# Attention row maxima: every third pair of score products split into two steps of 256 keys that share one bank, with the order written over two key tiles

## The chip, the core and the metric

The kernel runs on one core of one Trainium2 chip. The metric is the device time of one execution in microseconds (us). Engines are named as in the profile: PE is the matrix engine (PEld its weight loads), DVE the vector engine, ACT the scalar engine, POOL GpSimd, SP the engine whose queue issues nearly all DMAs.

## The reference

```python
x = A_x                                     # 1 x 2048 x 640, 32 heads of 20
x = x + A(layernorm(x))                     # attention: softmax(q k^T / sqrt(20)) v, then wo
x = x + B(layernorm(x))                     # squared ReLU MLP, 640 -> 1536 -> 640
x = x + A(layernorm(x))                     # the same weights again
x = x + B(layernorm(x))
```

All of it is float32. The softmax is the usual one: for each query row of each head the largest score over all 2048 keys is subtracted before the exponential. The kernel must therefore know the row maximum of every query before it forms that query's weights, and it forms every score twice: once to find the maxima, once to be exponentiated.

## The kernel before, in words

**Split numbers.** Inputs of most products are held as a rounded high part and the rest. For queries and keys three copies of the 20 numbers of a head stand below one another, so one product with a depth of 60 rows gives an accurate score. 60 rows fit into one half of the 128 rows of PE. One half (partitions 0 to 63) serves the even head of a pair, the other half (64 to 127) the odd head, and matmuls on the two halves run beside each other.

**Blocks and key tiles.** Attention goes over 32 blocks per layer (`NBLK`): 8 groups of 4 heads times 4 blocks of 512 queries. A block goes over 16 key tiles of 128 keys. For every key tile PE does

- four score products, depth 62, 128 keys by 512 queries (`score`, L565). The two rows beyond 60 carry the negative row maximum in two parts. ACT takes the exponential of each (L572) into a weights tile `e`;
- some products for maxima of a later block (`smax`, L493, with the matmul at L481): 128 queries by 512 keys. DVE reduces each bank to one column of `mx` (TENSOR_REDUCE, L493);
- the weighted sum (`pv`, L577): four heads side by side on 32 columns each, two passes each, accumulated in bank 7 over the 16 key tiles. It uses the weights of the key tile before the one whose scores have just been issued.

**Banks.** Scores rotate over banks 0 to 3, products for maxima over banks 4, 5 and 6 (`sm_ring`), the weighted sum has bank 7. A product for maxima waits until DVE has reduced what stood in its bank.

**At the end of a block** `finish` (L590) copies bank 7 out on DVE, and the reciprocal of the sums and the division follow on POOL. Once all maxima of a block are there, `mrows_max` (L525) takes the maximum over the columns of its `mx` tile, and `mrows` (L536) transposes the result. Both stand on DVE. POOL and SP then send the rows into the query tiles.

**The order.** Work on PE, DVE and ACT is issued in the order of a table, `ORDERS`, one string for eight key tiles, picked by the number of pairs of products for maxima that are due (`pairs`, 12 to 16; the same (query rows, keys) for both halves of the rows are a pair). In this program the string of 12 is picked all 62 times in each layer. Its letters: `a` and `b` are a score product on the lower and the upper half of the rows, `m` and `n` a product for maxima on the lower and the upper half, `V` the weighted sum. Eight key tiles hold 16 `a`, 16 `b`, 12 `m`, 12 `n` and 8 `V`. So between two `V` stand seven matmuls, four of them on one half of the rows and three on the other. The last block of a layer has no maxima left and is done in another way (`both_heads`, L1091).

**Before and between** stand the projections of q, k and v (`qkv`, with the first blocks' maxima), wo and the MLP, which the change leaves as they are.

A dependency that the framework does not see is added by `after(later, earlier)`. The projections already use it: where both halves of the rows add to one bank, a copy of one number on ACT (`mark_t`, L333) waits for the first half's last matmul, and the other half's first matmul waits for that copy.

Of the kernel before, what the change touches and what calls it, by code (L numbers as in the profile page):

```python
# [16 lines left out]
P = 128  # L17
# [7 lines left out]
QB = 512  # L25
NQB = S // QB
NG = H // 4
NKT = S // P
# [3 lines left out]
LEAST = -3.0e38  # L32
# [7 lines left out]
def tile_layers(  # L40
# [40 lines left out]
    banks = psum.tile([P, 8, 512], F32, tag="banks", name="banks")  # L81
# [215 lines left out]
    xt_, keys = {}, {}  # L297
# [125 lines left out]
    k_t, q_t, v_t, mx_t, kept = {}, {}, {}, {}, {}  # L423
# [46 lines left out]

    def maxima(t):
        if t not in mx_t:
            mx_t[t] = small.tile([P, 4, 4, 4], F32, tag="mx", bufs=14, name=name("mx"))
            if t in PARTLY:
                nc.vector.memset(mx_t[t], LEAST)
        return mx_t[t]

    def by_queries(dst, t, p, sub, c, par):

        b = 64 * par  # L480
        nc.tensor.matmul(  # L481
            dst,
            q_t[t][b : b + 60, p, sub * P : (sub + 1) * P],
            k_t[t // NQB, c][b : b + 60, p, :],
            start=True,
            stop=True,
        )

    def smax(ring, t, p, sub, c, par):

        dst = ring("sm")
        by_queries(dst, t, p, sub, c, par)
        nc.vector.tensor_reduce(  # L493
            maxima(t)[:, 2 * par + p, sub, c : c + 1], dst, axis=AX.X, op=ALU.max
        )

    def step_one(t, p, sub, x, par):
# [25 lines left out]
    def mrows_max(t):  # L523
        nm = nms[t % 2]
        nc.vector.tensor_reduce(  # L525
            nm[:, :16].rearrange("p (h s) -> p h s", h=4),
            mx_t.pop(t),
            axis=AX.X,
            op=ALU.max,
            negate=True,  # L530
        )
# [152 lines left out]
    def qkv(first, x_src, rest, scores):  # L684
# [275 lines left out]
        15: "anbmnanbaabmbnammbnaVbmbmmbVmbananVanmbanVnambmbVanbmnaVnmbaanVmbbanmV",  # L960
        14: "mbbbanmbbmambmVanannaVmbnaaanVbmabnmVanbmbmbVnaanmbVmabmbanVbmannaVn",
        13: "baanmbVmbanambbnbmVanbmnaVnaabnmbVanbmaanVnmbbanaVmnbmabVabbmmnaVm",
        12: "naambbmVanmbambVbmannabVnabnmabVabnmbanVbbmnanaVbmmbaanVbmbmnaaV",
    }

    def attention(first, x_src, first_rows):
# [1 line left out]
        es_of = {}  # L968
        e_n.clear()
        weights.extend(slot([P, 2, QB], F32, "e") for _ in range(6))  # L970
        st_n, sm_n = [0, 0], [0, 0]
        state = {"begun": -1, "done": 0, "acc": None, "debt": 0}
        sm_ring = Ring(4, 5, 6)
        todo = [
            (t, p, sub, c)
            for t in range(NBLK)
# [11 lines left out]
        ends = {x[0]: n for n, x in enumerate(todo)}  # L988
        blocks = sorted(ends)
        firsts = {todo[0][0]: 0, **{t: ends[s] + 1 for s, t in zip(blocks, blocks[1:])}}  # L990
        over = {t for t in range(NBLK) if t not in ends and t not in done}
        rows = {"next": min(t for t in range(NBLK) if t not in done), "at": None}

        def begin(i):

            t, u = divmod(i, NKT)
            g, qb = divmod(t, NQB)
            if u == 1:
                q_t.pop(t - 1, None)
                if t + 2 < NBLK and t + 2 not in q_t:  # L1000
                    load_q(t + 2)
            if u % 4 == 1 and qb == 0:
                k_t.pop((g - 1, u // 4), None)
                for h in (0, 1, 2, 3) if g else (0, 1, 2):
                    if g + h < NG and (g + h, u // 4) not in k_t:
                        load_k(g + h, u // 4, True)
                if g and g + 3 >= NG:
                    del kept[(g - 1) % 4, u // 4]
            if t == 1 and u % 4 == 1:
                load_k(3, u // 4, True)  # L1010
            if u in (2, 10) and qb == NQB - 1 and g + 1 < NG:
                load_v(g + 1, u // 8)
            if first and t < 16 and u % 6 == 3:
                prep_job()
            if first and t < 16 and u == 8:
                for sp in (w_o, w_1, w_2):
                    sp.save_full()
                    sp.past(sp.count, sp.got)
            if (t, u) in loads:
                loads[t, u]()  # L1020
            if t == NBLK - 1 and u == 12:
                first_rows.extend(row_tile(x_src, i) for i in range(4))
            if i in split:
                split.pop(i)()

        def op(o):
            if o in "ab":
                par = "ab".index(o)
                i, p = divmod(st_n[par], 2)
                if i >= last:  # L1030
                    return
                st_n[par] += 1
                if i > state["begun"]:
                    state["begun"] = i
                    begin(i)
                score(i // NKT, i % NKT, 2 * p + par, es_of.setdefault(i, {}))
            elif o in "mn":
                par = "mn".index(o)
                n = sm_n[par]
                if n == len(todo):  # L1040
                    return
                t, p, sub, c = todo[n]
                if n == firsts[t] and par == 0:
                    for s in blocks[blocks.index(t) :][:2]:
                        if s not in q_t:
                            load_q(s)
                if (t // NQB, c) not in k_t or t not in q_t:
                    return
                sm_n[par] += 1
                smax(sm_ring, t, p, sub, c, par)  # L1050
                if n == ends[t] and min(sm_n) > n:
                    over.add(t)
                    if t * NKT > state["begun"] + 2 * NKT:
                        del q_t[t]
# [46 lines left out]

        def pairs():

            n, i = min(sm_n), state["begun"] + 1
# [15 lines left out]
        spare = 0  # L1120
        while state["done"] < wide:
            for o in ORDERS[pairs()]:
# [3 lines left out]
                        both_heads(spare // 2 - 1)  # L1126
                else:
                    op(o)
        assert min(sm_n) == len(todo) and spare == 4
        for p in (0, 1, 0):  # L1130
            both_heads(p)
        while state["done"] < last:
# [360 lines left out]
```

## Time and profile before

| | |
|---|---|
| median of 3 runs | 3583.39 us (3582.76 to 3584.02) |
| profiled execution, span from first to last instruction | 3581.5 us |
| PE busy | 3569.0 us (100%) |
| DVE busy | 2753.5 us (77%) |
| ACT busy | 2647.3 us (74%) |
| POOL busy | 805.2 us (22%) |
| products for maxima (L481 on `k`), count | 3586 |
| reductions (L493), count | 3076 |
| attention's key tile loop, by the weighted sums' first and last start | 312.5 to 3174.0 us, in two stretches |

The profiled execution's own time is its span and the little that lies around it: the runs stand 1.3 to 2.5 us above the span. Attention fills two stretches, from about 310 to 1393 us and from about 2090 to 3174 us. Times of instructions in timeline rows are in us from the start of the span. A matmul's row begins with its weight load when that load is not hidden, and its end is modelled. Rows of DVE and ACT include the time in which a result is written out, while the next instruction has already begun.

### The profile page before, as it was taken

Reading aid. Unit: us, or ns where it says so; the run is one execution under the profiler, and the core shown is the slowest. Engines: PE = TensorE matmul, PEld = TensorE weight load, DVE = VectorE, ACT = ScalarE, POOL = GpSimd, SP = SyncE. Lnnn points to the kernel's source line nnn. Section 1 sums busy time; section 2 is a strip of 40 time slices with the busy share of each in tenths; the row PEclk is TensorE's granted clock in tenths of the full one; section 3 lists DMA queues with packets and bytes.
Section 4 is the critical chain, followed back from the end, with each engine's and each line's share of the span. In section 5 each row is a group of like instructions: output and inputs, shape, how many; then the busy total and the mean of one; then the engine's idle time right before and its main releaser. Section 6 shows DMA issues by size and latency. Waiting matters only on the chain.

```text
span 3581.5 us, 67667 instructions
## 1 busy us (share of the span) xinstructions
PE 3569.0 (100%) x25560; PEld 2121.6 (59%) x25560; DVE 2753.5 (77%) x5085; ACT 2647.3 (74%) x5146; POOL 805.2 (22%) x880
## 2 busy tenths in 40 slices
PE   9999999999999999999999999999999999999999
PEld 7896343333334335999988954333334433369998
DVE  8778999999999993455567789999999999824443
ACT  3778999999999995122237789999999999942221
POOL 6531434211211211111153201211211211211110
PEclk9999999999999999999999999999999999999999
DMA  9765555323211136834477652232232211367221
GB/s 305 274 230 167 168 157 155 105 69 81 57 44 51 46 95 204 262 99 115 134 275 244 192 149 70 62 81 60 66 79 54 52 39 45 112 216 248 74 80 39
DMA packets 377397, 452.58 MB, mean 126 GB/s; under 512 B 176642, under 2 KB 223746, under 8 KB 377070
## 3 DMA queue, kind: packets, MB, share of 16 engines
q1 hardware_dynamic: 376254, 445.89, 41.6%
q8 instruction: 201, 3.29, 0.4%
q10 hardware_dynamic: 816, 2.36, 0.2%
q14 instruction: 126, 1.03, 0.1%
HBM read 273.83 MB, written 174.30 MB: 125 GB/s over the span
## 4 chain that ended last, share of the span: by engine, by line
PE 96%; DVE 2%; DMA 1%; issue 0%; ACT 0%; POOL 0%; SPq 0%; ACTq 0%; DVEq 0%
PE banks L577 28%; PE banks L565 20%; PE banks L481 16%; PE banks L293 13%; PE banks L331 10%; PE banks L1259 9%; DVE mx L493 1%; PE banks L1091 1%; DMA q<-d_qk 0%; ACT e L1098 0%; DVE bst L244 0%; DVE xnT L257 0%; DVE x L252 0%; DMA d_qk<-ev 0%; PE banks L408 0%
## 5 line engine op out<-in xcount | busy, mean ns | idle before, releaser
L572 ACT ACTIVATE e<-banks 128x512 f32<-128x512 f32 x3968 | 2049.4, 604 | 61.1 <-PE banks L481 1.7
L493 DVE TENSOR_REDUCE mx<-banks 128x1 f32<-128x512 f32 x3076 | 1929.6, 683 | 208.4 <-PE banks L481 137.2
L481 PE MATMUL banks<-k,q 60*128 60x512 f32 x3586 | 1244.3, 427 | 1.0 <-DMA q<-d_qk 0.5
L565 PE MATMUL banks<-q,k 62*128 62x512 f32 x3968 | 1118.7, 434 | 0.4 <-DVE mx L510 0.4
L577 PE MATMUL banks<-e,vg 128*32 128x512 f32 x8192 | 1091.0, 605 | 1.5 <-ACT e L1098 1.5
L565 PEld LDWEIGHTS banks<-q,k 62*128 62x128 f32 x3968 | 584.4, 185 | 657.8 <-ACT e L572 625.6
L481 PEld LDWEIGHTS banks<-k,q 60*128 60x128 f32 x3586 | 582.0, 184 | 283.1 <-DVE mx L493 210.8
L510 DVE CUSTOM_DVE_ANT_0 rl<-banks,rl 128x512 f32<-128x512 f32 x510 | 332.6, 688 | 101.6 <-PE banks L481 91.0
L331 PE MATMUL banks<-xnT,wqk 64*128 64x512 f32 x2400 | 379.7, 394 | 0.3 <-ACT mark_t L333 0.3
L1244 ACT ACTIVATE r<-banks,b_t 128x512 f32<-128x512 f32 x96 | 66.2, 689 | 419.7 <-PE banks L293 418.3
L577 PEld LDWEIGHTS banks<-e,vg 128*32 128x32 f32 x8192 | 161.1, 108 | 360.2 <-issue 333.1
L502 ACT ACTIVATE rl<-banks 128x512 f32<-128x512 f32 x510 | 270.8, 597 | 98.9 <-PE banks L481 93.6
L1259 PE MATMUL banks<-w,h 128*128 128x320 f32 x2304 | 340.4, 309 | 0.0
L1259 PEld LDWEIGHTS banks<-w,h 128*128 128x128 f32 x2304 | 339.2, 188 | 1.2
L293 PE MATMUL banks<-xnT,w 128*128 128x512 f32 x1440 | 329.4, 389 | 0.0
L331 PEld LDWEIGHTS banks<-xnT,wqk 64*128 64x128 f32 x2400 | 286.4, 185 | 34.3 <-issue 2.4
L293 PEld LDWEIGHTS banks<-xnT,w 128*128 128x128 f32 x1440 | 269.6, 188 | 55.3
L271 POOL CAST mr<-nt 128x32 fp32r<-128x32 f32 x64 | 13.4, 209 | 1143.5 <-DVE nt L536 1143.5
L621 POOL TENSOR_TENSOR few<-few,minus_t 128x16 f32<-128x16 f32 x62 | 179.8, 2900 | 215.6 <-DMA few<-d_s 213.7
L331 PE MATMUL banks<-wv,xnT 64*128 64x320 f32 x1920 | 199.2, 307 | 0.9 <-ACT mark_t L333 0.9
L331 PEld LDWEIGHTS banks<-wv,xnT 64*128 64x128 f32 x1920 | 186.5, 185 | 2.7 <-ACT mark_t L333 1.4
L1245 DVE TENSOR_TENSOR r<-r 128x512 f32<-128x512 f32 x96 | 74.3, 774 | 124.0 <-ACT r L1244 124.0
(86 smaller groups left out, 2010.8 us busy)
## 6 DMA issues: line engine op xcount, KB each, us to landing
q<-d_qk SPq DMA_DIRECT2D x242, 240.0 KB
d_qk<-ev SPq DMA_DIRECT2D x80, 512.0 KB
k<-d_qk SPq DMA_DIRECT2D x152, 240.0 KB
x<-d_x SPq DMA_DIRECT2D x84, 320.0 KB
d_qk<-ev SPq DMA_DIRECT2D x80, 256.0 KB
d_o<-ot SPq DMA_DIRECT2D x248, 80.0 KB
ot<-d_o SPq DMA_DIRECT2D x38, 512.0 KB
d_v<-v SPq DMA_DIRECT2D x32, 512.0 KB
```

The costliest lines, as they stand in the source:

```text
L293: nc.tensor.matmul(dst, a, b, start=(n == 0), stop=(n == last))
L331: m = nc.tensor.matmul(ch["dst"][:, :width], *pair, start=first, stop=last)
L481: nc.tensor.matmul(dst, q_t[t][b : b + 60, p, sub * P : (sub + 1) * P], k_t[t // NQB, c][b : b + 60, p, :], start=True, stop=True,)
L493: nc.vector.tensor_reduce(maxima(t)[:, 2 * par + p, sub, c : c + 1], dst, axis=AX.X, op=ALU.max)
L502: nc.scalar.activation(res, dst, AF.Relu)
L510: nc.vector.tensor_tensor_reduce(out=r, in0=dst, in1=r, scale=1.0, scalar=LEAST, op0=ALU.add, op1=ALU.max, accum_out=maxima(t)[:, 2 * par ...
L565: nc.tensor.matmul(dst, k_t[t // NQB, kt // 4][b : b + 62, p, (kt % 4) * P : (kt % 4 + 1) * P], q_t[t][b : b + 62, p, :], start=True, stop ...
L572: nc.scalar.activation(es[p][:, par, :], dst, AF.Exp, scale=SCALE)
L577: nc.tensor.matmul(acc[32 * h : 32 * h + 32, :], v_t[t // NQB, kt // 8][:, kt % 8, 32 * h : 32 * h + 32], es[p][:, par, :], start=(kt == 0 ...
L621: nc.gpsimd.tensor_tensor(few, few, minus_t, op=ALU.pow)
L1245: nc.vector.tensor_mul(r, r, r)
L1259: nc.tensor.matmul(dst[:, :HALF], hs[f][:, hx, i * P : (i + 1) * P], w_2.piece(at_2(f0 + f, hw, hf)), start=(f == 0 and (hx, hw) == THREE[0]),
```

## The change

Of every three pairs of products for maxima two stay as they were, and the third is done in two steps (`u` and `w` in the table). Step one takes the first 256 keys, step two the last 256. In each step `u` puts the lower half's 128 x 256 product into the left half of a bank and `w` the upper half's into the right half of the same bank. Then one DVE reduction over 2 x 256 elements gives two columns of `mx`, one for each of the two heads. Matmuls on two halves of the rows must not write one bank at once, so a one-element memset on DVE (`done_t`, called mark below) waits for `u`, and `w` waits for the mark.

The string of 12 becomes four times a string over two key tiles. In the first of them stand u n a b a b m w, in the second b u a n m b a w: three and a half products of 512 columns on each half of the rows. The bank of `u` is held until `w`'s reduction is done and then goes to the end of the list `turn` of the three banks.

`mx` gets eight columns in place of four for each head and part of the rows, so `mrows_max` reduces 128 x 128 numbers in place of 128 x 64. The four new columns are set to a very small number by a memset on POOL (`two_columns`), called for a block and the one after it when the block's first product is taken up.

```diff
-            mx_t[t] = small.tile([P, 4, 4, 4], F32, tag="mx", bufs=14, name=name("mx"))
+            mx_t[t] = small.tile([P, 4, 4, 8], F32, tag="mx", bufs=14, name=name("mx"))
...
+    def two_columns(t):
+
+        if t not in halved:
+            halved.add(t)
+            nc.gpsimd.memset(maxima(t)[:, :, :, 4:], LEAST)
+
+    def smax_half(bank, t, p, sub, c, half, par, earlier=None):
+
+        w = QB // 2
+        dst = bank[:, par * w : (par + 1) * w]
+        m = by_queries(dst, t, p, sub, c, par, slice(half * w, (half + 1) * w))
+        if earlier is None:
+            mark = nc.vector.memset(done_t, 0.0)
+            after(mark, m)
+            return mark
+        after(m, earlier, "matmuls on two halves of the rows write to one bank in turn")
+        nc.vector.tensor_reduce(
+            maxima(t)[:, p : p + 3 : 2, sub, c + 4 * half],
+            bank.rearrange("q (r k) -> q r k", r=2),
+            axis=AX.X,
+            op=ALU.max,
+        )
...
-            mx_t.pop(t),
+            mx_t.pop(t)[:, :, :, : 8 if t in halved else 4],
...
-        12: "naambbmVanmbambVbmannabVnabnmabVabnmbanVbbmnanaVbmmbaanVbmbmnaaV",
+        12: "unababmwVbuanmbawV" * 4,
...
+            elif o == "u":
+                if parts or next_pair(parts):
+                    x = parts.pop(0)
+                    bank = turn.pop(0)
+                    opened.append((bank, x, smax_half(banks[:, bank, :], *x, 0)))
+            elif o == "w":
+                if opened:
+                    bank, x, mark = opened.pop()
+                    smax_half(banks[:, bank, :], *x, 1, mark)
+                    turn.append(bank)
+                    did(x[0])
```

How the instructions stand then. On PE, in the middle of the first layer's attention, two key tiles before; L565 are scores, L481 products for maxima, L577 the weighted sum:

```order
L481 MATMUL banks<-k_4704,q_12529 128x512
L565 MATMUL banks<-q_12607,k_4699 128x512 x2
L481 MATMUL banks<-k_4704,q_12529 128x512 x2
L565 MATMUL banks<-q_12607,k_4699 128x512 x2
L577 MATMUL banks<-e_4746,vg_12626 32x512 x2
L577 MATMUL banks<-e_4745,vg_12626 32x512 x2
L565 MATMUL banks<-q_12607,k_4699 128x512 x2
L481 MATMUL banks<-k_4704,q_12529 128x512 x2
L565 MATMUL banks<-q_12607,k_4699 128x512 x2
L481 MATMUL banks<-k_4704,q_12529 128x512
L577 MATMUL banks<-e_4748,vg_12626 32x512 x2
L577 MATMUL banks<-e_4747,vg_12626 32x512 x2
```

And two key tiles now, where L591 are scores, L603 the weighted sum, and L481 with 128x256 the two half products `u` and `w`:

```order
L481 MATMUL banks<-k_4788,q_11342 128x256
L481 MATMUL banks<-k_4788,q_11342 128x512
L591 MATMUL banks<-q_10840,k_4488 128x512 x4
L481 MATMUL banks<-k_4788,q_11342 128x512
L481 MATMUL banks<-k_4788,q_11342 128x256
L603 MATMUL banks<-e_4745,vg_10679 32x512 x2
L603 MATMUL banks<-e_4744,vg_10679 32x512 x2
L591 MATMUL banks<-q_10840,k_4488 128x512
L481 MATMUL banks<-k_4788,q_11342 128x256
L591 MATMUL banks<-q_10840,k_4488 128x512
L481 MATMUL banks<-k_4788,q_11342 128x512 x2
L591 MATMUL banks<-q_10840,k_4488 128x512 x2
```

Seven matmuls of 512 columns have become six of 512 and two of 256, and the last matmul ahead of the weighted sum is always `w`.

On DVE around the end of a block, before: L493 are the reductions, L590 is the copy of bank 7, L525 and L536 are the row maxima and their transposition of a later block.

```order
L493 TENSOR_REDUCE mx_7653<-banks 128x1 x36
L590 COPY o_7976<-banks 128x512
L493 TENSOR_REDUCE mx_7653<-banks 128x1 x12
L525 TENSOR_REDUCE nm_89<-mx_5770 128x16
L536 STREAM_TRANSPOSE nt_8068<-nm_89 128x32
L493 TENSOR_REDUCE mx_7653<-banks 128x1 x8
```

And now, around a copy (L616; L512 is the mark, L516 the reduction of a shared bank):

```order
L512 MEMSET done_t 1x1
L493 TENSOR_REDUCE mx_8431<-banks 128x1 x2
L516 TENSOR_REDUCE mx_8431<-banks 128x2
L616 COPY o_9382<-banks 128x512
L512 MEMSET done_t 1x1
L493 TENSOR_REDUCE mx_8431<-banks 128x1 x2
L516 TENSOR_REDUCE mx_8431<-banks 128x2
```

Per key tile DVE has three reductions as before, and a mark ahead of them. The mark stands directly behind the copy (and, four key tiles later, directly behind the row maxima and their transposition), ahead of the reductions of its key tile. There are 984 marks, 984 reductions of a shared bank and 2092 of the old kind in the program.

More of the change, by code (lines that the diff above doesn't have):

```diff
@@ L472, in maxima, with by_queries @@
         if t not in mx_t:
-            mx_t[t] = small.tile([P, 4, 4, 4], F32, tag="mx", bufs=14, name=name("mx"))
+            mx_t[t] = small.tile([P, 4, 4, 8], F32, tag="mx", bufs=14, name=name("mx"))
             if t in PARTLY:
-                nc.vector.memset(mx_t[t], LEAST)
+                nc.vector.memset(mx_t[t][:, :, :, :4], LEAST)
         return mx_t[t]
-    def by_queries(dst, t, p, sub, c, par):
+    def by_queries(dst, t, p, sub, c, par, keys=slice(0, QB)):
         b = 64 * par
-        nc.tensor.matmul(
+        return nc.tensor.matmul(
             dst,
             q_t[t][b : b + 60, p, sub * P : (sub + 1) * P],
-            k_t[t // NQB, c][b : b + 60, p, :],
+            k_t[t // NQB, c][b : b + 60, p, keys],
             start=True,
@@ L494, in smax @@
             maxima(t)[:, 2 * par + p, sub, c : c + 1], dst, axis=AX.X, op=ALU.max
+        )
+    halved = set()
+    done_t = cpool.tile([1, 1], F32, name="done_t")
+    def two_columns(t):
[16 more added lines that the diff above has]
+            op=ALU.max,
         )
@@ L970, in attention, with sm_ring @@
         weights.extend(slot([P, 2, QB], F32, "e") for _ in range(6))
-        st_n, sm_n = [0, 0], [0, 0]
+        st_n, sm_n = [0, 0], [0]
+        full, parts, opened = [[], []], [], []
+        halved.clear()
         state = {"begun": -1, "done": 0, "acc": None, "debt": 0}
-        sm_ring = Ring(4, 5, 6)
+        turn = [4, 5, 6]
+        def sm_ring(label):
+            return banks[:, turn[0], :]
         todo = [
@@ L991, in attention @@
         over = {t for t in range(NBLK) if t not in ends and t not in done}
+        to_do = {t: 2 * sum(x[0] == t for x in todo) for t in blocks}
         rows = {"next": min(t for t in range(NBLK) if t not in done), "at": None}
@@ L1024, in begin, with next_pair, did @@
                 split.pop(i)()
+        def next_pair(queues):
+            n = sm_n[0]
+            if n == len(todo):
+                return False
+            t, p, sub, c = todo[n]
+            if n == firsts[t]:
+                for s in blocks[blocks.index(t) :][:2]:
+                    if s not in q_t:
+                        load_q(s)
+                    two_columns(s)
+            if (t // NQB, c) not in k_t or t not in q_t:
+                return False
+            sm_n[0] += 1
+            if queues is parts:
+                parts.extend((t, p, sub, c, half) for half in range(2))
+            else:
+                for q in full:
+                    q.append((t, p, sub, c))
+            return True
+        def did(t):
+            to_do[t] -= 1
+            if not to_do[t]:
+                over.add(t)
+                if t * NKT > state["begun"] + 2 * NKT:
+                    del q_t[t]
         def op(o):
@@ L1038, in op @@
                 par = "mn".index(o)
[L1039 to L1054, printed above, removed]
+                if full[par] or next_pair(full):
+                    x = full[par].pop(0)
+                    smax(sm_ring, *x, par)
+                    turn.append(turn.pop(0))
+                    did(x[0])
[9 more added lines that the diff above has]
+                    turn.append(bank)
+                    did(x[0])
             else:
@@ L1102, in pairs @@
         def pairs():
-            n, i = min(sm_n), state["begun"] + 1
+            n, i = sm_n[0], state["begun"] + 1
             most = max(
@@ L1128, in attention @@
                     op(o)
-        assert min(sm_n) == len(todo) and spare == 4
+        assert sm_n[0] == len(todo) and not any(to_do.values()) and spare == 4
         for p in (0, 1, 0):
```

## The prediction, made before the changed kernel was run

> **What bounds the kernel now.** I read the page first, then the table of 100 us stretches, then the chain of waits inside attention, and at last the timeline of single key tiles. The page, with the share of each engine and the costliest groups (the two numbers behind the bar are busy us and mean ns of one):
>
> ```profile
> PE 3569.0 (100%) x25560; PEld 2121.6 (59%) x25560; DVE 2753.5 (77%) x5085; ACT 2647.3 (74%) x5146; POOL 805.2 (22%) x880
> ...
> PE 96%; DVE 2%; DMA 1%; issue 0%; ACT 0%; POOL 0%; SPq 0%; ACTq 0%; DVEq 0%
> ...
> L493 DVE TENSOR_REDUCE mx<-banks 128x1 f32<-128x512 f32 x3076 | 1929.6, 683 | 208.4 <-PE banks L481 137.2 <-PE banks L565 66.6 <-PE banks L331 0.2
> L1259 PE MATMUL banks<-w,h 128*128 128x320 f32 x2304 | 340.4, 309 | 0.0
> L293 PE MATMUL banks<-xnT,w 128*128 128x512 f32 x1440 | 329.4, 389 | 0.0
> ```
>
> The chain that ended last is PE's for 96% of the span. In attention the others are close behind, as this stretch shows (PE, PEld, DVE, ACT, POOL):
>
> ```profile
> 900.00:1000.00 100.00, 100.00 (x709) 39.79 (x705) 91.12 (x150) 97.26 (x189) 18.57 (x16) 1.00 0.24 61
> ```
>
> The chain of waits inside attention holds nothing but PE. The first and the last weighted sum of 22 key tiles:
>
> ```profile
> 1300.91 0.99 PE banks L577 x8
> ...
> 1347.66 0.55 PE banks L577
> ```
>
> (1347.66 - 1300.91) / 22 = 2.125 us for a key tile, with the copies and row maxima of block ends among them. The timeline of one key tile:
>
> ```profile
> 904.21 0.68 DVE L493 TENSOR_REDUCE mx<-banks 128x1 f32<-128x512 f32 x1
> 904.57 0.18 PEld L565 LDWEIGHTS banks<-q,k 62*128 62x128 f32 x1 [0.84 <-ACT e L572]
> 904.68 0.19 PEld L565 LDWEIGHTS banks<-q,k 62*128 62x128 f32 x1
> 904.91 0.39 PE L565 MATMUL banks<-q,k 62*128 62x512 f32 x1
> 904.95 0.18 PEld L481 LDWEIGHTS banks<-k,q 60*128 60x128 f32 x1
> 905.15 0.69 DVE L493 TENSOR_REDUCE mx<-banks 128x1 f32<-128x512 f32 x1 [0.25 <-PE banks L481]
> 905.15 0.40 PE L565 MATMUL banks<-q,k 62*128 62x512 f32 x1
> 905.70 0.16 PEld L577 LDWEIGHTS banks<-e,vg 128*32 128x32 f32 x8 [0.36 <-issue]
> 906.70 0.18 PEld L481 LDWEIGHTS banks<-k,q 60*128 60x128 f32 x1 [0.84 <-DVE mx L493]
> ```
>
> With 904.57 as zero: the first weights take 0.11 (the second load on that half starts at 904.68), then a half of the rows takes a matmul every 0.235 or so (904.68, 904.91, 905.15, so next 905.385). Four steps on the fuller half end at 1.05; the weighted sum starts at 1.13, 0.08 later, and the next key tile 1.00 after that. A product's reduction can start 0.58 after the key tile does (905.15), which is 0.225 behind the end of its step. And a bank is free 0.06 after the row of its reduction ends: 904.21 + 0.68 = 904.89, next load on it 904.95.
>
> So PE sets the time: seven matmuls take four steps, one half of a step on one half of the rows is empty. DVE has an idle 0.25 in a key tile, and its lateness goes nowhere as long as a bank is free in time. That is seen where a block ends. DVE's timeline there:
>
> ```profile
> 922.12 1.89 DVE L493 TENSOR_REDUCE mx<-banks 128x1 f32<-128x512 f32 x3 [0.25 <-PE banks L481]
> 923.92 0.68 DVE L590 COPY o<-banks 128x512 f32<-128x512 f32 x1
> 924.52 3.73 DVE L493 TENSOR_REDUCE mx<-banks 128x1 f32<-128x512 f32 x6
> ...
> 930.57 1.88 DVE L493 TENSOR_REDUCE mx<-banks 128x1 f32<-128x512 f32 x3 [0.20 <-PE banks L565]
> 932.37 0.21 DVE L525 TENSOR_REDUCE nm<-mx 128x16 f32<-128x64 f32 x1
> 932.68 0.21 DVE L536 STREAM_TRANSPOSE nt<-nm 128x32 f32<-128x32 f32 x1
> 932.92 1.89 DVE L493 TENSOR_REDUCE mx<-banks 128x1 f32<-128x512 f32 x3
> ```
>
> A reduction occupies DVE for 0.60 (1.89 for three, less the last one's 0.69, over two), the copy 0.60 (923.92 to 924.52), row maxima and transposition 0.55 (932.37 to 932.92). Both delay the reductions behind them; PE's 2.125 is not touched.
>
> **The change part by part.** All sums are differences against this profiled execution, whose span is 3581.5; the runs' median is 3583.39, and I add the sum to that.
>
> *The half products.* 320 columns take 340.4/2304 = 0.148, 512 take 329.4/1440 = 0.229, so a column is 0.00042 and 256 columns 0.121. Each key tile now has three steps and a half product on each half of the rows: 0.235 - 0.121 = 0.114 less, before any wait. The Trainium skill (TensorE: Matmul & The Clock Gate, Back-to-back issue gap) gives 262 cycles for 256 columns at 2.4 GHz, 0.109; by it the step saves 0.012 more, an estimate of 984 x 0.012 = 12 us, and the sum would be 3599. Two more weight loads in two key tiles are hidden: PEld is busy 39.79% here, and a load of 0.11 fits under a half product of 0.121. Without that cover each would show 0.11.
>
> *The bank that comes late.* In the first tile of the string the reductions are n, m, w: at 0.58, 1.18, 1.78. The last ends its row at 2.46 and frees its bank at 2.52, which is 0.51 after the second tile's start (2.125 - 0.114 = 2.01). The second tile's m takes just that bank, in A's order u, a, m, a: it could stream at 0.11 + 0.121 + 0.235 = 0.465, but its weights load only from 0.51, so it starts at 0.615. The a behind it, and the weighted sum, move by 0.15. Before, the third product of a tile came at a step where the same release was covered (load at 904.95, stream at 905.15). So a pair of tiles changes by -0.114 - 0.114 + 0.15 = -0.078. There are 984 marks, hence 492 pairs: -38 us.
>
> *The mark in the plain case.* u ends at 0.23, the mark can start at 0.455. A short memset on DVE, from the start of the program:
>
> ```profile
> 0.81 0.06 DVE L104 MEMSET eps_t<- 128x1 f32 x1 [0.81 <-PEq L1479]
> 0.84 0.06 DVE L106 MEMSET half_t<- 128x1 f32 x1
> ```
>
> 0.06, and 0.06 to release PE, as a reduction does: w's weights may load from 0.575, and are wanted at 0.705 (stream at 0.815, behind three matmuls less the half). Cover 0.13. The second tile's w reduction ends at about 0.81 + 3 x 0.60 = 2.61, which is 0.45 into the next first tile: DVE is only just free for that mark. No row has a mark on DVE that waits for PE; its bounds are 0.03 (the spacing of these two memsets) and the 0.185 us of the projections' mark on ACT (least, median and greatest ns):
>
> ```profile
> L333 ACT COPY mark_t<-mark_t x144: 172/185/192, 16.8 to 2085.9; 1x1 f32<-1x1 f32 x144
> ```
>
> I take 0.06 to 0.07, the memset's row, being the same operation.
>
> *The mark at block ends.* Queued behind a copy or a row maximum stand the mark, then the tile's reductions; w on PE waits for the mark, and behind w stands the weighted sum, so all of PE waits. With the copy in front the mark starts at 0.45 + 0.60 = 1.05, w's load at 1.17, its stream at 1.28 in place of 0.815: 0.46 late. That tile's reductions run late too: they free the second tile's bank 0.07 later than in the plain case. 0.53 for a copy. The row maxima now reduce 128 numbers in place of 64, by the reduction's 0.60/512 per number 0.07 more, so 0.62 in all and 0.55 on PE. Of the two layers' 64 blocks about 61 have each of them while maxima are still being made: 61 x (0.53 + 0.55) = +66 us. Before, this cost nothing.
>
> *POOL's memsets* of the new columns, some 64, lie on an engine 22% busy, a block (16 x 2.125 = 34 us) ahead of their use: nothing; at the two layer starts a few us at most.
>
> *ACT* needs about 4 x 0.49 = 1.96 a tile:
>
> ```profile
> 902.97 1.09 ACT L572 ACTIVATE e<-banks 128x512 f32<-128x512 f32 x2
> ```
>
> 1.09 less a row's 0.60 is 0.49 from one to the next. That is below 2.01, so it does not bind, but it would stop any gain beyond 0.165 a tile.
>
> Sum: -38 + 66 = +28 us: 3583 + 28 = 3611 us.
>
> A rule that speaks against the change: the Trainium skill (same page, "The cost: per-tile semaphore tail") says that increments of matmuls run after one another, 26.3 ns each. The change has one more incrementing matmul per tile, which by this would be 984 x 0.026 = 26 us more, an estimate from that page. The rows speak for less: steps with two incrementing matmuls take 0.235, those of L293, hardly any of which increment, 0.229, so 0.003 each.
>
> **The rivals.**
>
> *The lateness at block ends is absorbed (faster).* If w's wait were hidden, because DVE has caught up when u ends, only the -38 us stay: 3545. It decides if the copy and the row maxima come while DVE has over 0.5 of slack. Against it: DVE's rows show 0.20 to 0.25 idle in a tile of 2.125, and a tile of 2.01 has less. Chance 0.13.
>
> *The full half step (faster).* No bank is late and no mark: 984 x 0.114 = 112 us less, 3471. It needs banks freed 0.15 earlier than the row at 904.95 shows. 0.05.
>
> *Half of it (no change).* Block ends cost half of my price, 33 us: -5 us, 3578. That is within 0.2% (7.2 us), about what a measurement of this kernel can tell from no change. 0.14.
>
> *Dearer marks (slower still).* At ACT's 0.185 the mark ends 0.12 later, at 0.64, and n's reduction behind it starts 0.06 to 0.07 later; the late bank of each pair is that much later: 492 x 0.07 = 34 us more, 3643; or the 26 us of the page's rule, 3635. 0.12.
>
> The forecast has 0.56. Slower together 0.68, faster 0.18, same 0.14. The range 3552 to 3645 leaves out the full half step, most of the absorbed case, and a little above the dearer marks: some 0.19.
>
> **What would show it.** In the profile after: first tiles of 2.01 and second tiles of about 2.16 in the plain stretch, a mean near 2.085; behind each copy and each row maximum one tile of about 2.47, with w's load (L481, 256 columns) waiting for the mark; PEld idle "<- DVE done_t" some 50 us in all. Wrong, if tiles behind a copy take 2.1 or less, if second tiles take 2.01, or if the half product's step is far from 0.121. The mark's row on DVE should be near 0.06.

## The result, and the profile after

The changed kernel takes 3604.85 us (median of four runs, 3604.12 to 3605.45) beside 3583.07 us for the kernel before, a ratio of 1.0061 with a 95% interval of 1.0049 to 1.0073. It is slower by 21.8 us, where 28 were forecast. The span of its profiled execution is 3603.6 us.

The page after, for the engines, the chain and three groups (busy us, mean ns of one, then idle us ahead of it):

```profile
PE 3578.8 (99%) x26544; PEld 2146.4 (60%) x26544; DVE 2788.9 (77%) x6069; ACT 2610.9 (72%) x5146; POOL 810.6 (22%) x927
...
PE 91%; DVE 6%; DMA 1%; issue 1%; ACT 0%; POOL 0%; SPq 0%; DVEq 0%; ACTq 0%; POOLq 0%
...
L598 ACT ACTIVATE e<-banks 128x512 f32<-128x512 f32 x3968 | 2012.3, 605 | 118.7 <-PE banks L591 103.7
L493 DVE TENSOR_REDUCE mx<-banks 128x1 f32<-128x512 f32 x2092 | 1344.9, 686 | 91.2 <-PE banks L481 25.4
...
L516 DVE TENSOR_REDUCE mx<-banks 128x2 f32<-128x512 f32 x984 | 671.6, 682 | 1.2 <-PE banks L481 0.6
```

The same row of ACT in the page of the kernel before:

```profile
L572 ACT ACTIVATE e<-banks 128x512 f32<-128x512 f32 x3968 | 2049.4, 604 | 61.1 <-PE banks L481 1.7
```

DVE has come onto the chain (6%, before 2%), though its idle time ahead of reductions (91.2 + 1.2) and marks (107.9, below) is about what it was ahead of reductions before, 208.4. Less expected, ACT's idle time ahead of the exponentials has nearly doubled, 118.7 us in place of 61.1, and 103.7 of it is waiting for scores. The marks, from the groups by line with shapes apart, and PE's wait for them, from the waits (total us, times, longest):

```profile
L512 DVE MEMSET done_t<- 1x1 f32 x984 | 58.1, 59 | 107.9 <-PE banks L591 106.8 <-PE banks L481 1.0
```

```profile
PEld banks L481 <- DVE done_t L512: 44.8, 117, 0.9
```

A mark takes 59 ns. PE waits for marks 117 times (about two block ends in each of some 60 blocks), 44.8 us in all. The timeline of PE's weight loads over four key tiles (L603 is the weighted sum; a tile runs from 0.99 behind one weighted sum's start to 0.99 behind the next):

```profile
544.43 0.18 PEld L591 LDWEIGHTS banks<-q,k 62*128 62x128 f32 x1 [0.84 <-ACT e L598]
...
544.84 0.18 PEld L481 LDWEIGHTS banks<-k,q 60*128 60x128 f32 x1
...
545.54 0.16 PEld L603 LDWEIGHTS banks<-e,vg 128*32 128x32 f32 x8 [0.21 <-issue]
546.53 0.20 PEld L481 LDWEIGHTS banks<-k,q 60*128 60x128 f32 x2 [0.84 <-DVE mx L493]
...
547.64 0.16 PEld L603 LDWEIGHTS banks<-e,vg 128*32 128x32 f32 x8 [0.26 <-issue]
...
549.72 0.16 PEld L603 LDWEIGHTS banks<-e,vg 128*32 128x32 f32 x8 [0.20 <-issue]
550.72 0.21 PEld L481 LDWEIGHTS banks<-k,q 60*128 60x128 f32 x2 [0.84 <-DVE mx L493]
...
551.28 0.18 PEld L591 LDWEIGHTS banks<-q,k 62*128 62x128 f32 x1 [0.15 <-ACT e L598]
...
551.96 0.18 PEld L481 LDWEIGHTS banks<-k,q 60*128 60x128 f32 x1 [0.44 <-DVE done_t L512]
552.27 0.16 PEld L603 LDWEIGHTS banks<-e,vg 128*32 128x32 f32 x8
...
554.40 0.16 PEld L603 LDWEIGHTS banks<-e,vg 128*32 128x32 f32 x8 [0.25 <-issue]
```

From one weighted sum to the next: 2.10 and 2.08 in the plain tiles, 2.55 behind the copy, with the weight loads idle for 0.44 until the mark lets w's load go, then 2.13. DVE's timeline of the same stretch and of the row maxima after it:

```profile
544.10 0.69 DVE L516 TENSOR_REDUCE mx<-banks 128x2 f32<-128x512 f32 x1
545.03 0.06 DVE L512 MEMSET done_t<- 1x1 f32 x1 [0.24 <-PE banks L591]
545.21 1.29 DVE L493 TENSOR_REDUCE mx<-banks 128x1 f32<-128x512 f32 x2
...
551.21 0.68 DVE L616 COPY o<-banks 128x512 f32<-128x512 f32 x1
...
551.83 0.06 DVE L512 MEMSET done_t<- 1x1 f32 x1
...
560.04 0.28 DVE L551 TENSOR_REDUCE nm<-mx 128x16 f32<-128x128 f32 x1
560.35 0.21 DVE L562 STREAM_TRANSPOSE nt<-nm 128x32 f32<-128x32 f32 x1
560.49 0.69 DVE L493 TENSOR_REDUCE mx<-banks 128x1 f32<-128x512 f32 x1
560.51 0.06 DVE L512 MEMSET done_t<- 1x1 f32 x1
```

And ACT's timeline in the middle of a block; each row is a run of exponentials without a gap between their rows, here eight, that is two key tiles:

```profile
912.65 4.03 ACT L598 ACTIVATE e<-banks 128x512 f32<-128x512 f32 x8 [0.16 <-PE banks L591]
916.84 4.03 ACT L598 ACTIVATE e<-banks 128x512 f32<-128x512 f32 x8 [0.16 <-PE banks L591]
921.03 4.04 ACT L598 ACTIVATE e<-banks 128x512 f32<-128x512 f32 x8 [0.16 <-PE banks L591]
```

Two tiles take 4.19 (916.84 - 912.65), and ACT is idle for only 0.16 of that. One score, the first of a pair of tiles, comes to ACT 0.16 too late, and everything behind it runs without a gap. PE waits for ACT in return. In the plain first tiles of this trace (u n a b a b m w) the load of the fourth score starts 0.54 into the tile (median), 0.05 behind the end of an exponential's row; in the run both shorter, below, it starts at 0.42.

Over both layers, the sum of the change is then this (tile times here and in the table below are distances between weighted sums, good to about 0.01: means for plain tiles, with first and second tiles counted alike, and medians at block ends, where the means behind row maxima are up to 0.04 longer):

| | before | after | worked out |
|---|---|---|---|
| plain tile | 2.125 | 2.101 | 984 x -0.024 = -23 us |
| tile behind a copy | 2.110 | 2.54 | +0.44 over a plain one, +0.03 in the tile behind it |
| tile behind row maxima, and the next | 2.120, 2.125 | 2.358, 2.137 | +0.26 and +0.03 |
| block ends together | | | 61 x (0.47 + 0.29) = +46 us |

-23 + 46 = +23 us, measured 21.8. That they agree so closely is in part luck: the sum leaves out that the second tile behind a copy or row maxima takes only 2.05 to 2.06, some 5 us less in all. The first 495 tile distances of each layer, added up directly, give 2103.5 us before and 2123.1 after, 19.6 more; the rest of the difference lies outside them.

### The profile page after: what moved, and what is told of

It reads as the page before. It is cut to its first block, busy times and chain, and to the rows that moved or that the text cites. A ratio compares the mean times of both kernels' runs of the same rounds, so it can differ in the third digit from the quotient of the medians.

```text
span 3603.6 us, 70679 instructions
## 1 busy us (share of the span) xinstructions
PE 3578.8 (99%) x26544; PEld 2146.4 (60%) x26544; DVE 2788.9 (77%) x6069; ACT 2610.9 (72%) x5146; POOL 810.6 (22%) x927
## 3 DMA queue, kind: packets, MB, share of 16 engines
q10 hardware_dynamic: 816, 2.36, 0.2%
## 4 chain that ended last, share of the span: by engine, by line
PE 91%; DVE 6%; DMA 1%; issue 1%; ACT 0%; POOL 0%; SPq 0%; DVEq 0%; ACTq 0%; POOLq 0%
PE banks L603 27%; PE banks L591 16%; PE banks L481 16%; PE banks L293 13%; PE banks L331 10%; PE banks L1321 9%; DVE mx L493 2%; DVE mx L516 1%; DVE o L616 1%; DMA q<-d_qk 0%; DVE bst L244 0%; PE banks L1153 0%; SPq L76 0%; ACT e L1160 0%; DVE x L252 0%
## 5 line engine op out<-in xcount | busy, mean ns | idle before, releaser
L598 ACT ACTIVATE e<-banks 128x512 f32<-128x512 f32 x3968 | 2012.3, 605 | 118.7 <-PE banks L591 103.7
L493 DVE TENSOR_REDUCE mx<-banks 128x1 f32<-128x512 f32 x2092 | 1344.9, 686 | 91.2 <-PE banks L481 25.4
L481 PE MATMUL banks<-k,q 60*128 60x512 f32 x4570 | 1290.8, 391 | 12.6 <-DVE v L377 1.7
L603 PE MATMUL banks<-e,vg 128*32 128x512 f32 x8192 | 1091.0, 605 | 1.5 <-ACT e L1160 1.5
L591 PE MATMUL banks<-q,k 62*128 62x512 f32 x3968 | 995.8, 419 | 0.4 <-DVE mx L536 0.4
L481 PEld LDWEIGHTS banks<-k,q 60*128 60x128 f32 x4570 | 664.9, 184 | 543.4 <-DVE mx L493 412.7
L591 PEld LDWEIGHTS banks<-q,k 62*128 62x128 f32 x3968 | 563.4, 185 | 517.5 <-ACT e L598 423.3
L516 DVE TENSOR_REDUCE mx<-banks 128x2 f32<-128x512 f32 x984 | 671.6, 682 | 1.2 <-PE banks L481 0.6
L536 DVE CUSTOM_DVE_ANT_0 rl<-banks,rl 128x512 f32<-128x512 f32 x510 | 332.7, 689 | 101.6 <-PE banks L481 91.3
L603 PEld LDWEIGHTS banks<-e,vg 128*32 128x32 f32 x8192 | 161.1, 108 | 237.0 <-issue 216.5
```

Source lines behind the costliest of these rows:

```text
L481: return nc.tensor.matmul(dst, q_t[t][b : b + 60, p, sub * P : (sub + 1) * P], k_t[t // NQB, c][b : b + 60, p, keys], start=True, stop=True,)
L493: nc.vector.tensor_reduce(maxima(t)[:, 2 * par + p, sub, c : c + 1], dst, axis=AX.X, op=ALU.max)
L516: nc.vector.tensor_reduce(maxima(t)[:, p : p + 3 : 2, sub, c + 4 * half], bank.rearrange("q (r k) -> q r k", r=2), axis=AX.X, op=ALU.max,)
L536: nc.vector.tensor_tensor_reduce(out=r, in0=dst, in1=r, scale=1.0, scalar=LEAST, op0=ALU.add, op1=ALU.max, accum_out=maxima(t)[:, 2 * par ...
L591: nc.tensor.matmul(dst, k_t[t // NQB, kt // 4][b : b + 62, p, (kt % 4) * P : (kt % 4 + 1) * P], q_t[t][b : b + 62, p, :], start=True, stop ...
L598: nc.scalar.activation(es[p][:, par, :], dst, AF.Exp, scale=SCALE)
```

## The experiments

The profile shows that PE waits for marks, but not whether the mark is the cause. Three explanations were put against each other. **No slack**: DVE and ACT are both so nearly full that a bank which either gives back late holds PE up, and removing one wait uncovers the other. **The mark alone**: only DVE's marks at block ends stand in the way. **The half products themselves** cost more than whole ones. The first four kernels tell these apart; the later ones follow from what was seen. The table has all of them (us; ratios are against runs of the kernel before on the same chip, whose medians lay between 3582.60 and 3583.52, with the 95% interval):

| kernel | median | ratio | plain tile | behind copy | behind row maxima, next tile |
|---|---|---|---|---|---|
| after | 3604.85 | 1.0061 (1.0049 to 1.0073) | 2.101 | 2.54 | 2.358, 2.137 |
| order alone | 3615.81 | 1.0092 (1.0078 to 1.0106) | 2.153 | 2.187 | 2.187 |
| maxima behind the mark | 3605.22 | 1.0063 (1.0050 to 1.0076) | 2.103 | 2.535 | 2.084, 2.378 |
| exponentials shorter | 3583.92 | 1.0005 (0.9995 to 1.0014) | 2.076 | 2.52 | 2.36, 2.145 |
| reductions shorter | 3580.93 | 0.9995 (0.9986 to 1.0004) | 2.102 | 2.418 | 2.264, 2.018 |
| both shorter | 3517.61 | 0.9819 (0.9805 to 0.9832) | 2.02 | 2.424 | 2.266, 2.017 |
| before, both shorter | 3584.63 | 1.0006 (0.9996 to 1.0015) | 2.130 | 2.14 | 2.12 |
| tiles exchanged | 3576.12 | 0.9981 (0.9973 to 0.9990) | 2.100 | 2.329 | 2.173, 2.022 |
| order over one tile | 3567.77 | 0.9956 (0.9941 to 0.9971) | 2.071 | 2.50 | 2.347, 2.02 |
| order over eight tiles | 3562.02 | 0.9943 (0.9931 to 0.9956) | 2.091 | 2.265 | 2.158, 2.036 |

**Order alone.** The kernel before, with whole products in the order of the new string:

```diff
-        12: "naambbmVanmbambVbmannabVnabnmabVabnmbanVbbmnanaVbmmbaanVbmbmnaaV",
+        12: "nababmnVbmanmbaV" * 4,
```

> The kernel before with only its table changed: a string over two key tiles with whole products (n a b a b m n, then b m a n m b a), the nearest to the changed order without half products, marks or shared banks. If the loss comes from the halves, their marks and their shared bank, this stays near before: four steps a key tile, 2.125 us, 3583 us within 7 us. If the order over two tiles is itself the cause, because it asks for banks and scores earlier than they come free, it is slower by 15 to 25 us, 3598 to 3608, with key tiles that alternate between 2.12 and 2.16 us.

It is 33 us slower than the kernel before, more than the 15 to 25 expected for this case: an order over two tiles, as near to the new one as whole products allow, costs more than the whole change. With nearly the same order around them the half products gain 3615.81 - 3604.85 = 11 us. That speaks against the explanation that they are dearer than whole ones; it falls with the run both shorter, whose plain tiles with half products take 2.02. PE's loads show what the order costs; the first tile in these lines is b m a n m b a, the second n a b a b m n:

```profile
547.37 0.16 PEld L577 LDWEIGHTS banks<-e,vg 128*32 128x32 f32 x8 [0.36 <-issue]
...
548.90 0.18 PEld L565 LDWEIGHTS banks<-q,k 62*128 62x128 f32 x1 [0.24 <-ACT e L572]
...
549.56 0.16 PEld L577 LDWEIGHTS banks<-e,vg 128*32 128x32 f32 x8 [0.36 <-issue]
551.68 0.16 PEld L577 LDWEIGHTS banks<-e,vg 128*32 128x32 f32 x8 [0.36 <-issue]
```

The first takes 2.19, the second 2.12. A late score of the slow tile waits for a bank that ACT has still to read. DVE is not what holds it: it stands idle ahead of that tile's reductions, waiting for a product:

```profile
548.90 1.89 DVE L493 TENSOR_REDUCE mx<-banks 128x1 f32<-128x512 f32 x3 [0.20 <-PE banks L565]
```

A copy costs something here too, without any mark: the second tile behind it (not in the table) has a median of 2.257 in place of 2.12.

**Maxima behind the mark.** The row maxima and the transposition no longer stand ahead of the mark, but directly behind it:

```diff
-                    mrows_max(t)
-                    mrows(t)
+                    waiting.append(t)
...
                     opened.append((bank, x, smax_half(banks[:, bank, :], *x, 0)))
+                maxima_of_rows()
```

> The changed kernel with the row maxima and their transposition issued behind the next tile's mark in place of ahead of it; the copy of bank 7 stays. If w's wait for the mark behind them is the whole loss at a row maximum (a tile of 2.35 in place of 2.08 us, 61 times), this gains 15 to 17 us: 3588 to 3590. If DVE has simply no slack, the same lateness reaches PE one tile later through the bank that m waits for: the tile of 2.35 goes to about 2.05, the next one or two grow by the same 0.3, and the time stays at 3605 within 4 us.

Nothing was gained: 3605.22 beside 3604.85. On DVE the mark now stands at 561.40, at the start of the row maximum's row (by the kernel it is issued ahead of it), and the transposition comes behind it:

```profile
561.38 0.28 DVE L551 TENSOR_REDUCE nm<-mx 128x16 f32<-128x128 f32 x1
561.40 0.06 DVE L512 MEMSET done_t<- 1x1 f32 x1
561.70 0.21 DVE L562 STREAM_TRANSPOSE nt<-nm 128x32 f32<-128x32 f32 x1
561.83 1.25 DVE L493 TENSOR_REDUCE mx<-banks 128x1 f32<-128x512 f32 x2
562.99 0.68 DVE L516 TENSOR_REDUCE mx<-banks 128x2 f32<-128x512 f32 x1
```

The weighted sums of that kernel there, and the load of the next tile's m:

```profile
559.94 0.16 PEld L603 LDWEIGHTS banks<-e,vg 128*32 128x32 f32 x8 [0.23 <-issue]
562.04 0.16 PEld L603 LDWEIGHTS banks<-e,vg 128*32 128x32 f32 x8 [0.26 <-issue]
...
563.73 0.18 PEld L481 LDWEIGHTS banks<-k,q 60*128 60x128 f32 x1 [0.40 <-DVE done_t L512]
564.39 0.16 PEld L603 LDWEIGHTS banks<-e,vg 128*32 128x32 f32 x8 [0.36 <-issue]
566.41 0.16 PEld L603 LDWEIGHTS banks<-e,vg 128*32 128x32 f32 x8 [0.26 <-issue]
```

The tile with the mark is short now, 2.10, and the one behind it long, 2.35. The reductions behind the row maxima are late now, as the mark was before, and the next tile's m waits for their bank: its load starts at 563.73, 0.06 behind the end of the reduction of the shared bank (562.99 + 0.68 = 563.67). The view names a mark there because the next mark ends at about the same time. The mark alone falls as an explanation: DVE's time comes back at the next bank.

**Exponentials shorter.** ACT takes 448 of the 512 columns; the other weights are set to one at the start.

```diff
-        nc.scalar.activation(es[p][:, par, :], dst, AF.Exp, scale=SCALE)
+        nc.scalar.activation(es[p][:, par, :448], dst[:, :448], AF.Exp, scale=SCALE)
```

> The changed kernel with the exponentials of all blocks but the last over 448 of 512 queries (the other 64 weights stay at 1): ACT needs about 0.06 us less for each, all else is as it was. If plain tiles are held up by score banks that ACT frees late, pairs of tiles fall from 4.19 to about 4.12 us: 12 to 30 us less, 3575 to 3593. If they are held up only by the bank that DVE frees late, as the prediction had it, the time stays at 3605 within 5 us.

21 us less than the changed kernel. ACT is an engine that the prediction took not to bind. What is late next, in this kernel's loads:

```profile
542.21 0.16 PEld L603 LDWEIGHTS banks<-e,vg 128*32 128x32 f32 x8 [0.22 <-issue]
...
543.67 0.18 PEld L481 LDWEIGHTS banks<-k,q 60*128 60x128 f32 x1 [0.17 <-DVE mx L516]
...
544.32 0.16 PEld L603 LDWEIGHTS banks<-e,vg 128*32 128x32 f32 x8 [0.23 <-issue]
546.34 0.16 PEld L603 LDWEIGHTS banks<-e,vg 128*32 128x32 f32 x8 [0.22 <-issue]
```

The lines begin with a second tile, which takes 2.11; the first tile behind it takes 2.02. In the second the third load of a product for maxima (m) now shows a wait for DVE's shared bank. That is the late bank of the prediction.

**Reductions shorter.** DVE reduces 448 of 512 columns in each bank:

```diff
-            maxima(t)[:, 2 * par + p, sub, c : c + 1], dst, axis=AX.X, op=ALU.max
+            maxima(t)[:, 2 * par + p, sub, c : c + 1], dst[:, :448], axis=AX.X, op=ALU.max
...
-            bank.rearrange("q (r k) -> q r k", r=2),
+            bank.rearrange("q (r k) -> q r k", r=2)[:, :, :224],
```

> The changed kernel with every reduction of the key tile loop over 448 of 512 columns (64 scores are left out of each maximum): DVE needs about 0.067 us less for each of three a tile, 0.2 us a tile, all else is as it was. If DVE's lack of slack causes the loss at block ends and part of that in plain tiles, tiles behind a copy fall from 2.55 to about 2.33, behind a row maximum from 2.35 to about 2.2, plain tiles to 2.08: 25 to 40 us less, 3565 to 3580. If the wait is a fixed cost of the mark (its signals, not what stands before it on DVE), it stays above 3595.

24 us less, all of it around block ends (2.54 to 2.418, 2.358 to 2.264, and the next tile 2.137 to 2.018). A plain tile was expected to fall to 2.08 and is 2.102, as in the changed kernel; a pair is only divided otherwise, into 2.03 and 2.17, and the long tile waits for ACT:

```profile
543.57 0.16 PEld L603 LDWEIGHTS banks<-e,vg 128*32 128x32 f32 x8
...
545.19 0.18 PEld L591 LDWEIGHTS banks<-q,k 62*128 62x128 f32 x1 [0.21 <-ACT e L598]
...
545.74 0.16 PEld L603 LDWEIGHTS banks<-e,vg 128*32 128x32 f32 x8 [0.26 <-issue]
```

**Both shorter.** The two edits together.

> The changed kernel with exponentials over 448 of 512 queries (the other weights stay at 1) and reductions over 448 of 512 columns (those scores are left out of the maxima). If plain tiles are held up by both ACT's score banks and DVE's bank, each alone good for about the same loss, then taking both away gives what neither gave: both tiles at 2.01 to 2.03 us, and 60 to 75 us less than the changed kernel, 3530 to 3545. If the rest of the loss is PE's own (loads of half products, shared banks, more signals), it stays above 3560.

87 us less than the changed kernel, where the two apart gave 21 and 24, and more than the 60 to 75 expected: each covers the other. The weighted sums, with every plain tile at 2.02:

```profile
543.66 0.16 PEld L603 LDWEIGHTS banks<-e,vg 128*32 128x32 f32 x8
545.68 0.16 PEld L603 LDWEIGHTS banks<-e,vg 128*32 128x32 f32 x8
547.70 0.16 PEld L603 LDWEIGHTS banks<-e,vg 128*32 128x32 f32 x8 [0.25 <-issue]
```

So the half step itself is there: 2.125 - 2.02 = 0.105, forecast 0.114. Only the copies and row maxima still cost (2.424 and 2.266).

**Before, both shorter.** The same two cuts in the kernel before.

> The kernel before with the same two cuts as both_short: exponentials over 448 of 512 queries (the other weights stay at 1), reductions over 448 of 512 columns (those scores are left out of the maxima). If PE alone bounds the old loop, with its four steps, shorter ACT and DVE work changes nothing: 2.125 us a key tile, 3583 within 7 us, and the changed kernel's 87 us are a measure of waits that the change brought in. If the old loop was held by them as well, it falls below 3570.

No change: 3584.63 beside 3582.73, ratio 1.0006 (0.9996 to 1.0015). Before, neither engine held PE up. The waits that the cuts removed are waits that the change brought in.

**Tiles exchanged.** The same two tiles, the other one first:

```diff
-        12: "unababmwVbuanmbawV" * 4,
+        12: "buanmbawVunababmwV" * 4,
```

> The changed kernel with the two halves of its string exchanged (b u a n m b a w first, then u n a b a b m w). The two tiles follow one another as before, so plain tiles keep their mean of about 2.095 us; but the copy and the row maxima, which come at fixed even places, now stand ahead of the tile whose n is ready late (0.77 us after the tile's start in place of 0.54), where DVE has an idle stretch. If lateness of DVE is what block ends cost, tiles behind a copy fall from 2.55 to about 2.36 and behind a row maximum from 2.35 to about 2.23, with less carried on: 61 x 0.5 = 30 us less, about 3575, the range 3565 to 3590. If the cost of a block end is one wait that does not depend on the tile it falls into, the time stays at 3605 within 5 us.

29 us less than the changed kernel, and faster than the one before. The plain tile has not moved (2.100); the block ends have. The copy and the row maxima now fall into the tile b u a n m b a w, and the tiles behind them take 2.329 and 2.173 in place of 2.54 and 2.358. In that tile the mark waits for PE in any case (0.24 of DVE's idle time ahead of 545.03 in the changed kernel), so part of the copy fits in there; that this is the reason was not tried apart. Which of the two tiles a block ends in is worth 29 us, more than all that the plain tiles have gained (23).

**Order over one tile.** The mark's reduction and the scores at the same distance in every tile:

```diff
-        12: "unababmwVbuanmbawV" * 4,
+        12: "ubmbanawV" * 8,
```

> The changed kernel with one string for all key tiles, u b m b a n a w: m follows u at once, so its bank is wanted early but is one that has long been free, the fourth score stands last but one, and n comes late. By the times of the two traces so far (banks free 0.054 us behind a row's end, reductions of 0.60, exponentials of 0.478) plain tiles take 2.03 and 2.11 in turn, 2.07 in the mean, behind a copy 2.40, behind a row maximum 2.27: about 3570, the range 3560 to 3590. If the half products' own costs (marks, signals) are what eats the half step, no order helps and it stays at 3595 or more.

3567.77, here mostly by the plain tile (2.071); the block ends, expected at 2.40 and 2.27, are nearly as dear as in the changed kernel (2.50 and 2.347).

**Order over eight tiles.** Four kinds of tile; the copy and the row maxima fall into a tile u n a b m b a w, ahead of which stands u n a b a w m b:

```diff
-        12: "unababmwVbuanmbawV" * 4,
+        12: "unabmbawVubmbanawVubmbanawVunabawmbVunabmbawVubmbanawVbumbanawVunabawmbV",
```

> The changed kernel with a string of eight different key tiles, chosen so that the tiles ahead of which the copy and the row maxima stand want their mark late and their third bank late (u n a b m b a w, u b m b a n a w and u n a b a w m b mixed). By the durations and release times of the traces so far: plain tiles at 2.07 in the mean, behind a copy 2.27 in place of one_tile_order's 2.50, behind a row maximum 2.15 in place of 2.35: 3558 to 3566, against 3568 for one_tile_order. If the lateness only moves to the next tiles, it stays at 3568 within 4 us.

3562.02 us, ratio 0.9943 (0.9931 to 0.9956): the fastest full kernel of the case, 43 us below the changed one with the same instructions. Its weighted sums around a copy:

```profile
546.41 0.16 PEld L603 LDWEIGHTS banks<-e,vg 128*32 128x32 f32 x8 [0.26 <-issue]
548.68 0.16 PEld L603 LDWEIGHTS banks<-e,vg 128*32 128x32 f32 x8
550.69 0.16 PEld L603 LDWEIGHTS banks<-e,vg 128*32 128x32 f32 x8 [0.25 <-issue]
```

2.27 behind the copy, then 2.01. Whether a still better order exists was not tried.

## Why the prediction was right, and where its steps were off

The sign, the mechanism at the block ends and the sum held (+28 forecast, +21.8 measured). Two terms were mis-sized in opposite directions, -38 for -23 and +66 for +46, and part of the agreement is that these errors offset each other.

**The half products.** Forecast 0.114 less in a tile. With both other engines relieved 0.105 comes out. The prediction's second figure, 0.235 - 0.109 = 0.126, took the whole product from the rows and only the half product from the page. The Trainium skill (TensorE: Matmul & The Clock Gate, Back-to-back issue gap) gives 518 cycles for 512 columns and 262 for 256, so by the page alone the difference is 256 cycles or 0.107 at 2.4 GHz, an estimate from that page; the measured 0.105 agrees with it.

**The bank that comes late.** Forecast: plain pairs gain 0.078, -38 us. Measured: 2 x 0.024 = 0.048, -23 us. The late bank is real: the third load of L481 in the run exponentials shorter waits 0.17 for it. It is there in the changed kernel too, though the view marks no wait, since other loads keep PEld busy: the reduction ends at 544.10 + 0.69 = 544.79 and m's load starts at 544.84, 0.05 later, as it does throughout the plain second tiles of that trace. But the bank comes 0.41 into the second tile in place of 0.51, since the first tile is itself 0.09 late (2.10 against the forecast 2.01), so m's load is about 0.055 behind the 0.355 at which it was wanted, not 0.15. With ACT out of the way the late bank costs a pair 2 x (2.076 - 2.02) = 0.11.

**"It does not bind", of ACT.** This is the step that failed. 4 x 0.49 = 1.96 is below 2.01, but that compares an average with an average. The change also moved the first score of a pair of tiles behind u and n; ACT stands idle for 0.16 there, and then its 4.03 for eight exponentials make 4.19. The scores' banks come back late, and the first tile is 2.10. Order alone shows the wait by itself, exponentials shorter and both shorter show what it is worth: with DVE relieved and ACT not (reductions shorter) a pair loses 2 x (2.102 - 2.02) = 0.16, all that a plain pair of the changed kernel loses.

**The mark in the plain case.** Forecast hidden, with 0.06 for the memset: right on both. A mark's row is 59 ns and no plain tile's w waits for one. The cover is thinner than was worked out: in second tiles the mark starts at 545.03, 0.60 after the tile's start, not 0.455 (below).

**The mark at block ends.** Forecast 0.53 and 0.55. Behind a copy the mark starts 551.83 - 550.72 = 1.11 into the tile (forecast 1.05), and the tile takes 2.54 (forecast 2.47); measured from a plain tile that is itself longer than forecast, the two tiles give 0.47. The row maxima give 0.29: they hold DVE for 560.49 - 560.04 = 0.45, not 0.62, since the reduction behind the transposition begins 0.14 after it. PE's idle time for the marks is 44.8 us, forecast some 50.

**The increments.** The prediction gave 26 us to the rule of the Trainium skill (same page, "The cost: per-tile semaphore tail") as a dearer case. Both shorter has the eight matmuls with increments in a tile, and takes 2.02 where the rows gave 2.01: about 0.01 a tile could be theirs if the half step is worth the rows' 0.114, not 0.026.

**The rivals.** *Absorbed* fell: tiles behind a copy are 2.54. *The full half step* fell too, but both shorter shows it once the banks are early. *Dearer marks* fell with the mark's row of 59 ns (its two sums are 2 us low: 3611 + 34 = 3645 and 3611 + 26 = 3637). *Half of it* came nearest in its parts: the block ends cost two thirds of their price, and the plain gain fell short as well, so the time was not no change.

What stays open: how the 0.08 that a plain tile of the changed kernel stands above 2.02 divides between the two engines cannot be said, since each covers the other: relieving DVE alone takes nothing off it, relieving ACT alone 0.025, and both all of it. No run took the copy or the row maxima off DVE; that they are what block ends cost rests on the trace and on the runs that moved or shortened DVE's work.

## What to carry to other kernels

Where three engines are each over 90% busy in a stretch, an average per engine does not tell who binds: look at the order, at where each buffer is given back and how far ahead its next user stands. Cut each suspected engine's work alone and together; here the cuts alone gave 21 and 24 us and together 87, and a cut in the kernel before gave nothing. When a change alters both the work and the order, time the new order with the old work first: here it cost 33 us, more than the change as a whole, and another order of the same instructions turned +22 us into -21.

## What the runs showed that was not expected

**A short matmul's signal comes behind a longer one's.** In second tiles b (512 columns, other half of the rows) is issued just ahead of u (256 columns). By the rows of the prediction u's stream is done 0.23 after the tile's start, and its mark could begin at 0.455. It begins at 0.60 (545.03 - 544.43), and DVE's row names L591, the scores, as what released it. The eight-tile order has both cases in one trace. Where DVE stood idle and waited, the mark starts 0.44 behind the start of u's row when u stands first in its tile (median of 252 marks), and 0.59 behind it when b stands ahead of u (median of 121). That agrees with the Trainium skill (TensorE: Matmul & The Clock Gate, Part 3, The mechanism), by which matmuls packed into one array start and end in the order of the program. So splitting a product in two makes its first half available earlier only where no longer matmul stands just ahead.
